# A convolution, a 2-D Fourier filter and a gate on one core: transforms in quarters of PE's array, a ring of PSUM pairs, new engine sequences

## The chip, the cores and the metric

The kernel runs on one core of one Trainium2 chip. The metric is device time in microseconds (us), the median of some executions. A core has five engines that run side by side and wait for each other by semaphores: PE (TensorE, matrix products), VectorE (DVE), ScalarE (ACT), GpSimd (POOL) and SyncE (SP, which here only starts transfers). PE reads SBUF and writes PSUM, eight banks of 2 KB on each of 128 partitions. VectorE and ScalarE read PSUM; GpSimd does not touch it in this kernel.

## What is computed

```python
x = A_u                                             # 1 x 2048 x 640
g = sigmoid((x * gate_w).sum(-1, keepdims=True))
# a: a state space convolution along time
A = -exp(log_A_real) + 1j * A_imag;  C = (C_real + 1j * C_imag) * dt[:, None]
P = exp((A * dt[:, None])[:, :, None] * pos[None, None, :])
K = 2.0 * einsum("dn,dnl->dl", C, P).real           # 640 x 2048, N = 128
a = irfft(rfft(u, 4096) * rfft(K, 4096))[:2048] + u * D_skip
# b: a filter in the 2-D Fourier domain
b = irfft2(rfft2(x) * (w_r + 1j * w_i))
return g * a + (1 - g) * b
```

The kernel gets no array of x for b apart from A_u: both branches begin with the same transform of u along time.

## The kernel before

All transforms are matrix products with tables of cosines and sines, in float32. A transform of 4096 is done in two steps, 64 by 64 with 33 residues of the first step; the 640 channels go in four groups c of 160. The program has four parts.

*The transforms of u* (`phase_a`, first half). For each c and each half h of its channels, `stage1` (L530) takes 20 tiles u[128 rows = 4 channels x 32, 64] as the weights and a block-diagonal table e1 of 128 columns as what streams past; the result of 64 columns of the array goes to the upper or the lower half of PSUM's partitions. Copies bring it to SBUF (t1). `stage2` (L543) takes 160 columns of t1 through a table w2 with 128 rows and 64 columns, again in two halves. The result is copied and stored to memory (u_d), from where both branches read it back. Between these stand the gate's products (L617), four strips of 32 columns.

*The filter b* (second half of `phase_a`), in nine rounds of 128 rows (the last one 64): `front` loads and folds rows, `transposes` (L712) turns them, `channels` multiplies with tables by `quads` (L728 with 128 rows, L726 with the 33 that are left over), `filt` multiplies with the filter on VectorE, and `back1` (L728, L726; copies L785, additions L788 and L789) and `back2` (L797, copy L798) go back. The result is stored to s3e_d.

*The convolution's kernel K* (`phase_p`, then `phase_b`). `phase_p` works out parameters from log_A_real, A_imag and so on, in 640 columns on VectorE, ScalarE and GpSimd, splits each in three bfloat16 parts (`parts`, L451 and L453) and sends them through memory (par_d). `phase_b` takes 40 steps t; each has magnitudes (products L867, exponential L868), two groups of angles (products L876, sines L882 and L888; L888 writes back into PSUM), products of both on VectorE (L896 to L898) and GpSimd (L901, L902), and 64 products in strips of 32 columns (`kgen`, L915; copy L921). Exponential and sine need different tables on ScalarE, which an ACT_TABLE_LOAD brings in.

*The convolution* (`phase_c`, `phase_d`): for each c the two steps of the transform of K (L530, copies L531; L543), the complex product with u's transform (VectorE L1027, L1028; the sums on L1033, one half on VectorE and one on GpSimd), the way back (`backs`, L1058, copy L1060, store to s3_d), and the last step, `last_e` for b (L361, L1105) and `last_c` for a (L1119, then L1122 or L1124 and L1125), with the gate, to the output. For the last c `last_c` waits for a round trip through s3_d; eight products (L1152) that nobody reads stand before it on PE.

The order of the work is written out by hand: the program is recorded as a list of operations, and `ORDER`, a list of their numbers, sets in which order each engine gets its own. A tile's place in SBUF and PSUM is chosen when its first operation is written, as the slot that has been free for longest. Before, the filter has three single PSUM banks, K's part two pairs and a bank, the convolution three pairs and two single banks.

## Time and profile before

| | us |
|---|---|
| median of 3 runs (lowest, highest) | 541.96 (538.01, 542.72) |
| the profiled execution: time, span | 540.32, 538.5 |
| PE busy (share of the span) | 479.2 (89%) |
| VectorE busy | 432.6 (80%) |
| ScalarE busy | 310.0 (58%) |
| GpSimd busy | 294.7 (55%) |
| mean granted clock of PE | 0.946 |
| moved by DMA | 101.35 MB, 188 GB/s on average |

The profile is of one execution. PE stands for its products, PEld for loading weights beside them; recorded products overlap, so a busy PE is not PE at its peak. The clock is the part of PE's full clock that was granted. "Windows" give each engine's busy time in a stretch; "groups" put together the instructions of one source line, engine and shape; the chain of waits follows the work that ended last back from the end, in pieces of start, length, what and count. A float32 product of the program stands in the trace as two records, a bfloat16 one as one.

### The profile page before, as it was taken

The page shows a single profiled execution, that of the slowest core. Times are in us where ns is not written, and L with a number is a line of the kernel's source. Part 1 is how long each engine was busy: PE and PEld are TensorE (multiplying, and loading weights), DVE is VectorE, ACT ScalarE, POOL GpSimd, SP SyncE. Part 2 cuts the span into 40 slices and gives each one's busy share as a digit, 9 for nine tenths or more (in the row PEclk, how much of TensorE's full clock was granted, in tenths as well). Part 3 has the DMA queues.
Part 4 walks back from the last instruction along what each step waited for, and adds up shares of the span by engine and source line. Part 5 has one row for each costly group of instructions (what it writes and reads, how often), then busy time and mean ns, then how long its engine had stood idle before and what let it go on. Part 6 is the DMA issues. An engine that isn't in the chain of part 4 may idle for free.

```text
span 538.5 us, 17006 instructions
## 1 busy us (share of the span) xinstructions
PE 479.2 (89%) x7288; PEld 370.3 (69%) x7288; DVE 432.6 (80%) x678; ACT 310.0 (58%) x486; POOL 294.7 (55%) x318
## 2 busy tenths in 40 slices
PE   8988999776989779997899988797899999999996
PEld 6977998554766556664676655566789878889651
DVE  4988687888898898999978987525499887999973
ACT  4682304789786878888698866866423414332110
POOL 3487430865845782763937416516455648568670
PEclk9999999779799989999899996858999999999999
DMA  8845788514126504162031360195437799799996
GB/s 328 298 179 193 274 305 279 180 51 133 51 100 191 157 27 133 37 227 87 27 103 43 110 177 1 51 367 199 147 122 254 249 393 330 248 344 280 334 302 219
DMA packets 48658, 101.35 MB, mean 188 GB/s; under 512 B 3908, under 2 KB 33368, under 8 KB 46536
## 3 DMA queue, kind: packets, MB, share of 16 engines
q1 hardware_dynamic: 25464, 67.41, 35.8%
q10 hardware_dynamic: 20080, 22.55, 13.0%
q0 software_dynamic: 3040, 10.33, 5.7%
q8 instruction: 57, 0.93, 0.7%
q14 instruction: 17, 0.14, 0.1%
HBM read 60.94 MB, written 39.65 MB: 187 GB/s over the span
## 4 chain that ended last, share of the span: by engine, by line
PE 40%; DVE 8%; ACT 7%; POOL 6%; issue 4%; DMA 3%; DVEq 0%; ACTq 0%; POOLq 0%; SPq 0%
PE psum L530 7%; PE psum L543 6%; PE psum L1058 5%; PE psum L728 5%; PE psum L915 3%; PE psum L726 3%; ACT sbuf L868 3%; PE psum L361 2%; PE psum L797 2%; PE psum L1119 2%; PE psum L876 2%; POOL sbuf L901 2%; DMA sbuf<-s3e_d 2%; ACT sbuf L882 1%; DVE sbuf L1033 1%
## 5 line engine op out<-in xcount | busy, mean ns | idle before, releaser
L543 PE MATMUL psum<-sbuf,sbuf 128*64 128x160 f32 x1056 | 87.0, 304 | 0.3 <-DVE sbuf L578 0.3
L530 PE MATMUL psum<-sbuf,sbuf 128*64 128x128 f32 x1280 | 80.1, 279 | 3.5 <-DVE sbuf L578 1.9
L530 PEld LDWEIGHTS psum<-sbuf,sbuf 128*64 128x64 f32 x1280 | 74.7, 140 | 10.2 <-issue 4.4
L543 PEld LDWEIGHTS psum<-sbuf,sbuf 128*64 128x64 f32 x1056 | 76.2, 135 | 7.4 <-issue 3.6
L1033 POOL TENSOR_TENSOR sbuf<-sbuf 64x320 f32<-64x320 f32 (+1 forms) x68 | 62.3, 918 | 33.8 <-DVE sbuf L1028 17.2
L868 ACT ACTIVATE sbuf<-psum 128x1024 f32<-128x1024 f32 (+1 forms) x80 | 61.8, 827 | 28.1 <-PE psum L867 28.0
L902 POOL TENSOR_TENSOR sbuf<-sbuf 128x512 f32<-128x512 f32 x40 | 53.6, 1342 | 34.2 <-ACT sbuf L882 23.5
L728 PE MATMUL psum<-sbuf 128*128 128x160 f32 (+3 forms) x280 | 60.1, 334 | 4.8 <-DVE sbuf L788 3.0
L901 POOL TENSOR_TENSOR sbuf<-sbuf 128x512 f32<-128x512 f32 x40 | 57.1, 1432 | 12.4 <-ACT sbuf L882 12.4
L898 DVE TENSOR_TENSOR sbuf<-sbuf,psum 128x1024 f32<-128x1024 f32 x40 | 48.6, 1215 | 15.8 <-ACT psum L888 15.7
L728 PEld LDWEIGHTS psum<-sbuf 128*128 128x128 f32 (+1 forms) x280 | 41.2, 191 | 20.6 <-issue 12.6
L915 PE MATMUL psum<-sbuf 128*32 128x64 f32 x2560 | 50.7, 238 | 5.2 <-ACT sbuf L921 1.6
L915 PEld LDWEIGHTS psum<-sbuf 128*32 128x32 f32 x2560 | 43.4, 121 | 15.7 <-issue 9.1
L1060 ACT COPY sbuf<-psum 128x640 f32<-128x640 f32 x32 | 22.2, 693 | 48.8 <-PE psum L1058 41.2
L531 ACT COPY sbuf<-psum 128x512 f32<-128x512 f32 x40 | 24.7, 623 | 43.4 <-PE psum L530 43.3
L1033 DVE TENSOR_TENSOR sbuf<-sbuf 64x320 f32<-64x320 f32 (+1 forms) x68 | 48.2, 715 | 1.1
L876 PE MATMUL psum<-sbuf 64*128 64x256 bf16 x320 | 32.6, 295 | 16.3 <-ACT sbuf L882 10.7
L888 ACT ACTIVATE psum<-psum 128x1024 f32<-128x1024 f32 x40 | 40.6, 1015 | 6.8 <-PE psum L876 6.6
L1058 PE MATMUL psum<-sbuf 128*64 128x160 f32 x528 | 42.3, 300 | 1.2 <-DVE sbuf L1033 1.1
L882 ACT ACTIVATE sbuf<-psum 128x1024 f32<-128x1024 f32 x40 | 41.0, 1026 | 3.3 <-PE psum L876 2.5
L1058 PEld LDWEIGHTS psum<-sbuf 128*64 128x64 f32 x528 | 36.7, 136 | 4.8 <-DVE sbuf L1033 1.5
L578 DVE COPY sbuf<-psum 128x320 f32<-128x320 f32 (+2 forms) x54 | 29.9, 563 | 10.4 <-PE psum L530 6.2
(145 smaller groups left out, 878.5 us busy)
## 6 DMA issues: line engine op xcount, KB each, us to landing
u_d<-sbuf SPq DMA_DIRECT2D x32, 320.0 KB, 4.5
sbuf<-u_d ACTq DMA_DIRECT2D x16, 640.0 KB, 6.5
s_d<-sbuf ACTq DMA_DIRECT2D x15, 640.0 KB, 6.2
sbuf<-s_d SPq DMA_DIRECT2D x6, 1280.0 KB, 9.3
sbuf<-in_w_l SPq DMA_DIRECT2D x8, 642.0 KB, 3.8
sbuf<-u_d SPq DMA_DIRECT2D x8, 640.0 KB, 5.1
k_d<-sbuf SPq DMA_DIRECT2D x4, 1280.0 KB, 5.7
sbuf<-k_d SPq DMA_DIRECT2D x8, 640.0 KB, 4.2
```

Source lines behind the costliest of these rows:

```text
L530: nc.tensor.matmul(p[64 * ri:64 * ri + 64, j, :], src(i + j), e1[ri], start=True, stop=True)
L543: ins = nc.tensor.matmul(p[64 * j:64 * j + 64, i, 160 * ri:160 * ri + 160], w2[:, x, 64 * ri:64 * ri + 64], t1[:, x // 2 if x < 32 else K0 ...
L728: P.matmul(out, src(c), tab[0], start=first, stop=not first)
L868: st.exp = S.activation(ef[:, :, c:c + n], p[:, :, 0:n], AF.Exp)
L876: P.matmul(p[:, j, n * g:n * g + n], pars[0][t][x, g], rp[x, c:c + n], start=True, stop=True)
L882: S.activation(sc.rearrange("p d v i -> p (d v i)"), p.rearrange("p j w -> p (j w)"), AF.Sin, scale=TWO_PI)
L898: V.tensor_tensor(out=x[:, 0].rearrange("p d (h j) -> p d h j", h=2), in0=e[:, :, 0:64].rearrange("p d (h j) -> p d h j", h=2), in1=cx.uns ...
L901: G.tensor_tensor(out=y[:, 1], in0=e[:, :, 64:96], in1=sc[:, 0], op=ALU.mult)
L902: G.tensor_tensor(out=y[:, 0], in0=e[:, :, 64:96], in1=sc[:, 1], op=ALU.mult)
L915: P.matmul(st.pb[32 * r:32 * r + 32, o, :], y[:, ri, 4 * qq + JR[r], :], x[:, ri, 4 * qq + JR[r], :], start=t % 2 + qq + 1 - ri == 0, stop ...
L1033: return eng.tensor_tensor(out=t2[64 * im:64 * im + 64, o, :], in0=m[l, :hn, 0, :], in1=m[l, :hn, 1, :], op=ALU.add if im else ALU.subtract)
L1058: T.mm = P.matmul(p[x:x + 64, i // 2, 160 * (i % 2):160 * (i % 2) + 160], T.w3[:, k0 + h + i, x:x + 64], t2[:, h + i, :], start=True, stop ...
```

## The change

- `stage1`: the weights are 64 rows (two pairs of channels, not four channels), what streams past is 64 columns of e1 without the zero blocks. Four products, for two row halves and two column halves, stand next to each other: the quarters of the array. Row halves write different banks of a pair. One copy takes up to 1024 columns.
- `stage2` and `backs`: 64 rows in place of 128, the real and the imaginary part one after the other into the same PSUM, four quarters next to each other. In `fronts` the complex product's sums are formed on all 128 partitions, the real part on VectorE, the imaginary part on GpSimd.
- `last_e`, `last_c`: 64 rows and 32 columns, eight products next to each other, without the zero blocks.
- The filter: three chunks of 64 rows in two halves in place of 128 and 33, all products, transposes and the way back with row halves. `back1` multiplies both rows at once, its copies take 644 columns, and the additions of L788 and L789 come after `back2`, as two operations of 640 columns a round.
- PSUM: until the convolution begins one pool of three pairs of banks serves everything, with two single banks for K and the gate; the convolution has four pairs.
- `phase_p`: GpSimd's operations go to VectorE, the casts to ScalarE; the gate's weights (L590) to VectorE.
- 221 products of 128 columns of weights by 128 columns and 52 of 32 by 128, into a PSUM bank that nobody reads, are put between others on PE by the order (`SPARE`).
- A new `ORDER`. The host lays out inputs and tables to match.

```diff
-    for i in range(0, nq, 4):
-        n = min(4, nq - i)
-        p = ps.tile([128, 4, 128], F32, tag="ps", name="p_s1")
-        for j in range(n):
-            for ri in range(2):
-                nc.tensor.matmul(p[64 * ri:64 * ri + 64, j, :], src(i + j), e1[ri], start=True, stop=True)
+    for i in range(0, 20, 8):
+        n = min(8, 20 - i)
+        p = pair(T, "p_s1")
+        for q in range(n):
+            for h in range(2):
+                r = slice(64 * h, 64 * h + 64)
+                for y in range(2):
+                    nc.tensor.matmul(p[64 * y:64 * y + 64, h, 64 * q:64 * q + 64], src[r, i + q, :], T.e1[y][r], start=True, stop=True)
...
+    for ro in range(2):
         for ri in range(2):
-            for j in range(nl // 64):
...
+                    nc.tensor.matmul(p[64 * j:64 * j + 64, y, 160 * ro:160 * ro + 160], T.w2[r, pr // 2, j, ri, ro, :],
+                                     t1[r, 2 * (pr // 2) + j if x < 32 else K0 // 2, :, ri], start=not ri or x == 32, stop=ri == 1 or x == K0)
...
+        def products(st, src, w, xs, name):
+            p = pair(T, name)
+            for i, x in enumerate(xs):
+                for k in range(3):
+                    for c in range(2):
+                        r = slice(64 * c, 64 * c + 64)
+                        P.matmul(p[:st.nl, c, 161 * i:161 * i + 161], src[r, k, x, 0:st.nl], td[r, w, k, :], start=k == 0, stop=k == 2)
...
-                eng.tensor_copy(t[:, j], v[:, :, :])
+                S.copy(t[:, j], v[:, :, :])
...
+            V.tensor_tensor(out=t2[:nl, x, 0], in0=ma[:nl, :hn, 0], in1=ma[:nl, :hn, 1], op=ALU.subtract)
+            G.tensor_tensor(out=t2[:nl, x, 1], in0=mb[:nl, :hn, 0], in1=mb[:nl, :hn, 1], op=ALU.add)
...
+        p = pair(T, name)
+        for j in range(2):
+            r = slice(64 * j, 64 * j + 64)
+            for g in range(4):
+                P.matmul(p[32 * g:32 * g + 32, j, 0:160 * n], w(g)[r], t3[r, a0(g):a0(g) + n], start=True, stop=True)
...
+        spare = T.p1.tile([128, 2, 128], F32, tag="pg", name="p_f")
+        for i, (cols, count) in enumerate(SPARE):
+            for _ in range(count):
+                for x in range(0, 128, cols):
+                    nc.tensor.matmul(spare[x:x + cols, i, :], c1[:, x:x + cols], c1[:, 128:256], start=True, stop=True)
...
+SPARE = (128, 221), (32, 13)
```

What the new order does is seen on the engines. PE in the filter's part; before, two calls of `quads` follow each other (L728 with 128 rows, L726 with 33):

```order
L728 MATMUL psum_72<-sbuf_68 128x160
L728 MATMUL psum_72<-sbuf_68 128x161
L726 MATMUL psum_72<-sbuf_68 128x160
L726 MATMUL psum_72<-sbuf_68 128x161
L726 MATMUL psum_72<-sbuf_68 128x160
L726 MATMUL psum_72<-sbuf_68 128x161
L728 MATMUL psum_72<-sbuf_68 128x160
L728 MATMUL psum_72<-sbuf_68 128x161 x2
L728 MATMUL psum_72<-sbuf_68 128x160
```

and after the change (L695 are the filter's products, L863 K's strips, L816 the magnitudes, L399 the unread products):

```order
L695 MATMUL psum_72<-sbuf_68 128x161 x12
L399 MATMUL psum_72<-sbuf_66 128x128
L863 MATMUL psum_72<-sbuf_68 32x64 x32
L816 LDWEIGHTS sbuf_67
L816 MATMUL psum_72<-sbuf_67 128x512
L816 LDWEIGHTS sbuf_67
L816 MATMUL psum_72<-sbuf_67 128x512
L399 MATMUL psum_72<-sbuf_66 128x128 x2
L695 MATMUL psum_72<-sbuf_68 128x161 x12
```

A call of `products` is one run of twelve in one mode of the array, and unread products in another mode stand between what had stood side by side.

ScalarE in the middle of K's steps, before (L882 and L888 are sines, L868 exponentials, the others copies):

```order
L882 ACTIVATE sbuf_68<-psum_72 128x1024
L785 COPY sbuf_68<-psum_72 128x160
L785 COPY sbuf_68<-psum_72 128x161
L888 ACTIVATE psum_72<-psum_72 128x1024
L882 ACTIVATE sbuf_68<-psum_72 128x1024
L921 COPY sbuf_67<-psum_72 128x512
L746 COPY sbuf_68<-psum_72 128x2x160
L746 COPY sbuf_68<-psum_72 128x2x161
L888 ACTIVATE psum_72<-psum_72 128x1024
L868 ACT_TABLE_LOAD
L868 ACTIVATE sbuf_68<-psum_72 128x2x512
```

and after (L830 and L836 are sines, L817 exponentials):

```order
L836 ACT_TABLE_LOAD
L836 ACTIVATE psum_72<-psum_72 128x1024
L830 ACTIVATE sbuf_68<-psum_72 128x1024
L738 COPY sbuf_68<-psum_72 128x644
L836 ACTIVATE psum_72<-psum_72 128x1024
L817 ACT_TABLE_LOAD
L817 ACTIVATE sbuf_68<-psum_72 128x2x512
L753 COPY sbuf_68<-psum_72 128x644
L817 ACTIVATE sbuf_68<-psum_72 128x2x256
L868 COPY sbuf_67<-psum_72 128x512
L836 ACT_TABLE_LOAD
```

Sines and exponentials stood in long runs and now alternate: the program has 45 table loads on the lines of exponential and sine where it had 18, and the copies are fewer and longer. In the changed order K's last steps and the filter's last round also stand side by side to the end, where before five of K's steps came after the filter.

## Prediction

> **What bounds the kernel now.** I read the windows first, cut at the three places where the work changes its kind: the transforms of u (to 96 us), the filter and the kernel K side by side (96 to 380), the convolution (380 to 520), and the way out. Each row gives the busy time of PE, weight load, VectorE, ScalarE and GpSimd, then PE's granted clock, the DMA share and GB/s.

> ```profile
> span 538.5 us, 17006 instructions
> DMA  8845788514126504162031360195437799799996
> 0.00:96.00 96.00, 87.79 (x1524) 79.95 (x1525) 70.62 (x112) 42.75 (x79) 44.81 (x48) 1.00 0.75 267
> 96.00:380.00 284.00, 243.75 (x3879) 171.31 (x3879) 231.44 (x365) 223.03 (x339) 162.16 (x174) 0.90 0.35 114
> 380.00:520.00 140.00, 134.25 (x1858) 114.35 (x1848) 122.37 (x182) 43.57 (x70) 84.56 (x95) 1.00 0.82 278
> 520.00:538.50 18.50, 13.46 (x50) 4.71 (x48) 8.21 (x20) 0.63 (x1) 3.15 (x3) 0.99 0.69 240
> 96.00:345.00 249.00, 214.27 (x3435) 148.92 (x3435) 220.52 (x349) 199.05 (x304) 151.02 (x163) 0.92 0.31 98
> 345.00:380.00 35.00, 29.49 (x456) 22.39 (x452) 10.92 (x16) 23.99 (x36) 11.14 (x11) 0.73 0.61 229
> ```

> Stages 1 and 3 are PE's: 91% and 96% busy, nothing else above 87%. Stage 2 is nobody's alone: to 345 us VectorE is busiest with 220.5 of 249 (89%), PE 86%, ScalarE 80%, and its last 35 us, when the filter has ended and K has not, keep VectorE at 31%. In stage 3 transfers take 0.82 of the DMA engines, and in the slices from about 430 us on the DMA digits are mostly 9, so they stand right behind PE.

> PE's real cost of a product is the cadence in the chain of waits (start, length, what, count), since recorded ends overlap. The groups give the counts; a float32 product of the program is two records.

> ```profile
> 390.22 0.87 PE psum L530 x16
> 391.09 1.61 PE psum L361 x8
> 392.70 1.14 PE psum L543 x16
> 393.84 1.09 PE psum L1058 x16
> 268.52 1.27 PE psum L797 x4
> 278.56 0.74 PE psum L728 x4
> 279.30 0.75 PE psum L726 x8
> 272.41 1.03 PE psum L915 x64
> L543 PE MATMUL psum<-sbuf,sbuf 128*64 128x160 f32 x1056 | 87.0, 304 | 0.3 <-DVE sbuf L578 0.3
> L530 PE MATMUL psum<-sbuf,sbuf 128*64 128x128 f32 x1280 | 80.1, 279 | 3.5 <-DVE sbuf L578 1.9 <-ACT sbuf L578 1.6
> L1058 PE MATMUL psum<-sbuf 128*64 128x160 f32 x528 | 42.3, 300 | 1.2 <-DVE sbuf L1033 1.1
> L361 PE MATMUL psum<-sbuf,sbuf 128*64 128x480 f32 (+1 forms) x96 | 20.3, 523 | 0.6 <-DMA sbuf<-s3e_d 0.6
> L1119 PE MATMUL psum<-sbuf,sbuf 128*64 128x480 f32 (+1 forms) x96 | 21.2, 528 | 2.7 <-DVE sbuf L1033 1.1 <-DVE sbuf L1122 0.5 <-DVE sbuf L1105 0.5
> ```

> So 54.4 ns each for L530, 71 for L543, 68 for L1058, 201 for L361 with 480 columns. L728 fills the array with 160 columns, L797 with 320: the second 160 columns cost 0.53 us for four, 0.13 each, and 0.21 us of a block of L728 is left for coming into its mode. L726 uses half the rows: two run at once, 94 ns. L915 uses 32 columns of the array: four run at once, 16.1 ns for 64 columns. Halves by rows and strips by columns thus run together here; no row shows both at once.

> **The change, part by part.** *First transforms in quarters* (L530, now line 525). The block-diagonal right side went, half of which was zeros: 2560 records of 64 columns take the place of 1280 of 128. Nearest row: L915, four at once, 64 columns, 16.1 ns. 2560 x 16.1 = 41.2 us against 1280 x 54.4 = 69.6: 28.4 less, half in stage 1 and half behind it. *Second transforms and the way back* (L543, L1058) do the same arithmetic in twice as many halves: 2048 at 35.5 = 72.7 against 75.0, and 1040 at 34 = 35.4 against 35.9; 2.8 less. *Last transforms* (L361, L1119) drop zeros too: eight at once in place of two, 384 records, 128 in each group at 50 ns and 64 at 33.5, 17.1 against 34.3 (64 x 201 + 32 x 135, twice): 17.2 less. Bounds for these: if four quarters take f times the time I give them, the four lines make 149.3 f + 17.1 against 214.8, so from f = 1.32 on PE gains nothing. I take f = 1, as L726 and L915 both do all that their share of the array allows.

> Stage 1 has 14.2 + 1.2 = 15.4 us less on PE. Its transfers need 0.75 x 96 = 72 us, which is under 80, so they cut a part only: I take 12, bounds 0 and 15.4. Stage 3 has 14.2 + 1.2 + 0.5 + 17.2 = 33 less: 107 on PE. But its transfers are 0.82 x 140 = 115 us of the DMA engines, with the same bytes, and at its start little can be moved. I take 124, 16 less; bounds 6 less (they stay at the digits of 430 to 513 us, where little room is left) and 33. VectorE, 122 of the 140 us now, would stand in the way at 124, but this part is halved too: 68 operations on 64 partitions become 36 on 128 with the same columns, and GpSimd's like them.

> ```profile
> L1033 DVE TENSOR_TENSOR sbuf<-sbuf 64x320 f32<-64x320 f32 (+1 forms) x68 | 48.2, 715 | 1.1
> ```

> 36 x 0.715 = 26 against 48: VectorE keeps 100 us. The last 18.5 us, a round trip through memory and the last products, stay.

> *Parameters off GpSimd.* A subtraction of 640 columns costs GpSimd 1.6 us and VectorE 0.9; the casts go to ScalarE. They lie in stage 1, where VectorE has 25 us free and ScalarE 53.

> ```profile
> L453 POOL TENSOR_TENSOR sbuf<-sbuf,sbuf 128x640 f32<-128x640 f32 (+1 forms) x4 | 6.3, 1575 | 0.3
> L453 DVE TENSOR_TENSOR sbuf<-sbuf 128x640 f32<-128x640 f32 (+1 forms) x4 | 3.4, 865 | 0.0
> 63.33 3.20 POOL L856 DMA_DIRECT2D sbuf<-par_d  x6 [3.85 <-DMA par_d<-sbuf]
> 80.08 0.50 PE L867 MATMUL psum<-sbuf 48*128 48x512 bf16 x4
> ```

> The parameters are read back from 63 us and first used at 80, 17 us of cover. A stage that is 12 shorter eats most of it, and the quicker chain gives some back: nothing, with 5 us as the upper bound.

> *Filter in 64-row halves.* Products: 280 + 280 records become 864 of L726's kind, 57 us (66 ns without the block's 0.21) against 55.6, so no gain in arithmetic. But the two sorts no longer alternate: with transposes and the way back in the same mode, stage 2 has 85 changes of mode against 271, before the unread products are added. VectorE loses 68 small operations and gets 18 of 640 columns:

> ```profile
> L788 DVE SCALAR_TENSOR_TENSOR sbuf<-sbuf,sbuf,psum 128x160 f32<-128x160 f32 x34 | 12.3, 376 | 12.3 <-ACT sbuf L785 11.7 <-PE psum L797 0.5
> L789 DVE SCALAR_TENSOR_TENSOR sbuf<-sbuf,sbuf,psum 128x160 f32<-128x160 f32 x34 | 12.1, 376 | 4.8 <-ACT sbuf L785 4.0 <-PE psum L876 0.8
> L1028 DVE TENSOR_TENSOR sbuf<-psum,sbuf 128x640 f32<-128x640 f32 (+1 forms) x36 | 28.0, 779 | 4.6 <-PE psum L543 4.3
> ```

> 18 x 0.78 = 14 against 24.4; the rest of its filter handles about as many columns as before. VectorE: 231 - 10 = 221.

> *New sequences.* ScalarE's order is where they cost. Exponentials and sines each need their own table, and the order now alternates far more: 45 table loads (22 + 6 + 17) against 18.

> ```profile
> L868 ACT ACT_TABLE_LOAD x8 | 10.3, 1283 | 1.4 <-PE psum L867 1.3
> L882 ACT ACT_TABLE_LOAD x6 | 7.7, 1283 | 0.3 <-PE psum L876 0.3
> L888 ACT ACT_TABLE_LOAD x4 | 5.1, 1283 | 0.1
> L715 ACT COPY sbuf<-psum 128x512 f32<-128x512 f32 (+3 forms) x27 | 15.0, 587 | 3.7 <-PE psum L712 3.7
> L717 ACT COPY sbuf<-psum 128x512 f32<-128x512 f32 (+3 forms) x27 | 15.0, 576 | 4.1 <-PE psum L712 3.7
> L746 ACT COPY sbuf<-psum 128x320 f32<-128x320 f32 (+3 forms) x18 | 7.7, 430 | 6.3 <-PE psum L728 6.1
> L785 ACT COPY sbuf<-psum 128x160 f32<-128x160 f32 (+1 forms) x34 | 9.2, 296 | 16.3 <-PE psum L728 16.3
> L798 ACT COPY sbuf<-psum 128x320 f32<-128x320 f32 x34 | 14.1, 434 | 4.9 <-PE psum L797 4.7
> L882 ACT ACTIVATE sbuf<-psum 128x1024 f32<-128x1024 f32 x40 | 41.0, 1026 | 3.3 <-PE psum L876 2.5
> L1060 ACT COPY sbuf<-psum 128x640 f32<-128x640 f32 x32 | 22.2, 693 | 48.8 <-PE psum L1058 41.2
> ```

> 27 x 1.283 = 34.6 us more. The filter's copies are 61.0 us now and become, a round, two of 1024 columns (1.03), two of 512 (0.59) and four of 644 (0.69): 6.0, nine times 54, 7 less. ScalarE in stage 2: 223 + 35 - 7 = 251 us, and it becomes the busiest engine there. At the 89% that VectorE reached, 251 / 0.89 = 282. The filter's rounds now end with K's last steps, so the thin 35 us go; that gain is what pays for the loads. Stage 2: 2 less, bounds 33 less (ScalarE never waits) and 28 more (loads and copies all on the path).

> *Unread products*: 442 records of 128 columns at 0.106 us and 104 at a quarter of it, 50 us, in 65 places of PE's order; 114 changes of mode come with them, 199 in all, still 72 fewer than before, 15 us at 0.21. PE in stage 2: 244 + 50 - 15 - 5 (first transforms that stand there) + 1 = 275 of 282. They cost nothing only while PE would have waited, and it is idle for 40 us there now. Behind each stand, in PE's order, products that ScalarE waits for. Against that stands the clock: 0.73 in the last 35 us, 0.90 over the stage. [...] I take 0.

> *PSUM ring*: three pairs of banks serve about 250 uses in stage 2, 3.4 us for a use at 282 us; a block of PE (0.75) and a copy (0.7 to 1.03) hold a pair for 1.8. Taken at 0; from 1.6 us of extra holding on it would bound, with no room left.

> The sum: 540.3 us (the profiled execution; its span is 538.5, the median of the three times 541.96) - 12 - 2 - 16 = 510.

> **Rivals.** *A, transfers don't hold PE* in stages 1 and 3: all of 15.4 and 33 arrives, 540.3 - 48.4 - 2 = 490. For it: the digits leave room before 430 us. Against: the 9s behind it. *B, the table loads lie bare*: stage 2 grows by 28 in place of losing 2, 540. For: ScalarE runs in order, at 251 of 284 us. Against: its 61 idle us. *C, the unread products fall on the path*: 275 of work and the 40 of waiting, stage 2 takes 315, 31 more than now, 543. For: ten in a row are 2 us ahead of a wanted product. Against: they stand where waits were expected. *D, four quarters run only two at a time* (the change doesn't do what it says): f = 2, PE's four lines take 316 for 214.8, 101 more, 640; it decides from f = 1.32 and is the slower one. Against: L726 and L915. For: no row has both splits.

> **How the numbers follow.** Forecast 0.55, A 0.20, B 0.12, C 0.08, D 0.05. Forecast and A are faster by over 1% (about what a measurement can tell), B and C lie at no change, a quarter of them to either side: faster 0.80, same 0.10, slower 0.10. The range runs from 485, a little below A since ScalarE's load allows more, to 535, short of B and C: what it leaves out is most of B and C, D, and a part of A. The forecast's own range is 497 to 524.

> **What would show it.** Line 525 at about 16 ns a record in the chain, 541 at 35; DMA digits of 9 through stage 3 and PE under 90% there; ScalarE over 85% in stage 2 with 45 loads; first angles some 10 us earlier. Wrong if stage 2 is under 265 or over 300 us, or if stage 3 falls below 115.

## The result and the profile after

The kernel after the change takes 584.7 us (median of four executions, 582.4 to 588.6) against 540.0 (536.9 to 542.7): ratio 1.084, 95% interval 1.075 to 1.093. It is 45 us slower; the forecast was 30 us faster. The profiled execution took 588.6 us, its span is 586.5. From its page: the busy tenths of PE, PE's clock and the DMA engines in 40 slices.

```profile
span 586.5 us, 24840 instructions
PE   6886978999998978899998998966888669687692
PEclk9888899999999799999999999988899969988887
DMA  8666468433226305151214123584966989999995
```

PE had 7s to 9s nearly everywhere before; now it has 6s in the first slices and, from slice 27 of the 40 on, 6s again and again, mostly beside DMA digits of 8 and 9. The same windows as in the prediction (PE, weight load, VectorE, ScalarE, GpSimd, PE's clock, DMA share, GB/s), cut where the three stages meet:

```profile
0.00:89.00 89.00, 69.00 (x2365) 61.60 (x2369) 45.89 (x75) 44.73 (x64) 10.63 (x24) 0.90 0.65 226
89.00:385.00 296.00, 271.41 (x5258) 215.55 (x5252) 245.08 (x326) 254.48 (x301) 156.71 (x148) 0.99 0.36 114
385.00:586.00 201.00, 145.70 (x3772) 115.39 (x3760) 99.15 (x149) 43.06 (x60) 56.59 (x59) 0.88 0.85 238
```

From here on the stages are cut at two events that every trace has, the first sine of K's steps and the end of the last one, and "the end" is what follows the last product of the way back. All in us:

| kernel | stage 1 | stage 2 | stage 3 | of it the end |
|---|---|---|---|---|
| before | 97.5 | 283.9 | 157.2 | 19.7 |
| after | 90.7 | 295.0 | 200.8 | 28.8 |

So stage 1 gave 7, stage 2 lost 11, stage 3 lost 44. Stage 3 is not longer because PE has more to do: it is busy for 146 of 201 us. Its clock is lower, too: 0.90 and 0.88 in stages 1 and 3, where it had been 1.00. Added up, PE stands at half clock for 17 us of stage 1 and 48 of stage 3, where it had been 0 and under 1, and most of these stretches begin in or just behind a pause (391.2 to 398.0 us, 408.2 to 411.7, 466.3 to 479.9).

**Two things show in stage 3.** The first is in the groups of PE and in the chain of waits (start, length, what).

```profile
L541 PE MATMUL psum<-sbuf,sbuf 64*64 64x160 f32 x2048 | 103.9, 321 | 21.6 <-issue 20.4
L525 PE MATMUL psum<-sbuf,sbuf 64*64 64x64 f32 x2560 | 57.4, 239 | 27.3 <-issue 22.1
```

```profile
402.69 1.21 PE psum L525 x80
403.89 4.28 issue
408.18 0.58 PE psum L525 x12
408.76 0.08 PE psum L541
408.86 3.64 PE psum L541 x62
```

PE stops for 4.3 us in the middle of a run of the same products and waits for nothing that the profile knows ("issue"). The before lines of these products had 0.3 and 3.5 us of idle time, none of it "issue". What PE waits for shows in the DMA queue of kind "instruction", q8 (packets, MB, share of the DMA engines' time). First the page of the kernel before, then after:

```profile
q1 hardware_dynamic: 25464, 67.41, 35.8%
q8 instruction: 57, 0.93, 0.7%
```

```profile
q1 hardware_dynamic: 26120, 67.36, 37.8%
q8 instruction: 89, 1.46, 1.1%
```

After, PE has 11374 products (counted here and below as records of the trace, of which a float32 product is two) and as many weight loads, 22748 instructions; 1.46 MB is 64 bytes for each, and a packet of 16 KB holds 256, that is 128 products. Before it is the same sum: 14576 instructions, 57 packets. By this sum I take these packets to be PE's own program. Set beside six of PE's pauses, from the packets and the records of the trace after (us; PE stops where the last record before the pause starts):

```
PE stops   resumes   a packet of q8 starts, lands   landed before PE resumes
 388.31    393.48      391.09      392.06             1.41
 403.68    408.18      405.67      406.58             1.59
 418.55    420.99      418.33      419.71             1.28
 463.96    469.91      467.14      468.45             1.46
 510.27    514.72      512.11      513.45             1.27
 543.11    547.88      544.95      546.30             1.58
```

Counting every pause of 0.6 us or more that ends 1.15 to 1.75 us behind such a landing: 19 us in stage 1 and 42 us in stage 3, against 0 and 1 in the kernel before. The places fit as well: from one of these pauses to the next in stage 3 PE works through 127 or 128 products or about a whole multiple (255, 510, 765); 15 of the 16 pauses stand so. Two packets never start closer than 3.39 us in this trace, that is 26.5 ns for each of its 128 products (3.42 us before, and 3.22 in wide_tiles, the closest pair of any run). The quarters of line 525 follow each other at 18.4 ns within a run: they use up 128 in 2.4 us, faster than any two packets came. I call this **theory F**, fetches.

The long pauses need more than that. In five of the six above the packet starts only 1.8 to 3.2 us after PE has stopped, and 7 to 11 us behind the packet before it. In these stretches the DMA engines are busy for 0.83 or more with other transfers. So the packet may be waiting behind them; no run shows that by itself.

The second is in the transfers: q1 above moved the same 67.4 MB in 222 us of the 16 engines' time (37.8% of 586.5) instead of 193. The DMA issues (KB each, median us to landing), before and after:

```profile
sbuf<-s_d SPq DMA_DIRECT2D x6, 1280.0 KB, 9.3
```

```profile
sbuf<-s_d SPq DMA_DIRECT2D x6, 1280.0 KB, 18.3
```

These are the loads of `load_c`. The change cut them, and those of `load_e`, by partitions, which the diff shown above leaves out:

```diff
-        nc.sync.dma_start(t3es[c][:, :, :], T.s3e_d[c].rearrange("k (r a) d -> (k r) a d", r=4))
+        for g in range(4):
+            nc.sync.dma_start(t3es[c][32 * g:32 * g + 32], T.s3e_d[c, :, 16 * g:16 * g + 16])
...
-            for x in range(2):
-                nc.sync.dma_start(t3[:, x], src[:, x])
+            for j in range(2):
+                nc.sync.dma_start(t3[64 * j:64 * j + 64], T.s3_d[c, :, 32 * j:32 * j + 32])
```

Their packets of 10 KB took 426 ns on average before and 641 after, those of 20 KB (10 KB twice) 1443. In stage 3 q1 and q10, the queues of SP and ScalarE, took 161 us of the engines' time instead of 119. Not all of that is slower packets: behind K's last sine these queues start 44.3 MB of transfers, and 40.2 before, since some that stood ahead of it (a load of s3e_d among them) now come later. This is **theory T**, transfers. **Theory U** is what the prediction doubted in stage 2: unread products or table loads.

### The profile page after: what moved, and what is told of

Same layout as the page of the kernel before. It is cut to its first block, busy times and chain, and to the rows that moved or that the text cites. A ratio compares the mean times of both kernels' runs of the same rounds, so it can differ in the third digit from the quotient of the medians.

```text
span 586.5 us, 24840 instructions
## 1 busy us (share of the span) xinstructions
PE 486.1 (83%) x11374; PEld 392.5 (67%) x11374; DVE 390.1 (67%) x548; ACT 342.3 (58%) x424; POOL 223.9 (38%) x231
## 3 DMA queue, kind: packets, MB, share of 16 engines
q1 hardware_dynamic: 26120, 67.36, 37.8%
q8 instruction: 89, 1.46, 1.1%
## 5 line engine op out<-in xcount | busy, mean ns | idle before, releaser
L541 PE MATMUL psum<-sbuf,sbuf 64*64 64x160 f32 x2048 | 103.9, 321 | 21.6 <-issue 20.4
L541 PEld LDWEIGHTS psum<-sbuf,sbuf 64*64 64x64 f32 x2048 | 83.9, 140 | 34.2 <-issue 26.4
L525 PE MATMUL psum<-sbuf,sbuf 64*64 64x64 f32 x2560 | 57.4, 239 | 27.3 <-issue 22.1
L525 PEld LDWEIGHTS psum<-sbuf,sbuf 64*64 64x64 f32 x2560 | 54.3, 152 | 31.2 <-issue 23.5
L695 PE MATMUL psum<-sbuf 64*128 64x161 f32 (+1 forms) x864 | 69.1, 307 | 2.7 <-ACT sbuf L817 0.8
L399 PE MATMUL psum<-sbuf 128*128 128x128 f32 (+1 forms) x546 | 69.3, 286 | 0.0
L695 PEld LDWEIGHTS psum<-sbuf 64*128 64x128 f32 (+1 forms) x864 | 61.7, 184 | 8.7 <-ACT sbuf L817 2.3
L817 ACT ACTIVATE sbuf<-psum 128x1024 f32<-128x1024 f32 (+1 forms) x80 | 62.0, 817 | 5.6 <-PE psum L816 5.1
L399 PEld LDWEIGHTS psum<-sbuf 128*128 128x128 f32 (+1 forms) x546 | 56.5, 175 | 10.5 <-issue 8.6
L978 PE MATMUL psum<-sbuf 64*64 64x160 f32 x1040 | 51.1, 312 | 4.4 <-issue 3.2
L957 DVE TENSOR_TENSOR sbuf<-psum,sbuf 128x640 f32<-128x640 f32 (+1 forms) x36 | 27.9, 778 | 38.4 <-PE psum L541 32.1
L958 DVE TENSOR_TENSOR sbuf<-psum,sbuf 128x640 f32<-128x640 f32 (+1 forms) x36 | 28.1, 780 | 37.7 <-PE psum L541 22.6
L575 ACT COPY sbuf<-psum 128x1024 f32<-128x1024 f32 (+3 forms) x42 | 33.1, 808 | 31.7 <-PE psum L525 17.8
L863 PE MATMUL psum<-sbuf 128*32 128x64 f32 x2560 | 46.8, 226 | 3.0 <-POOL sbuf L850 1.1
L978 PEld LDWEIGHTS psum<-sbuf 64*64 64x64 f32 x1040 | 41.7, 139 | 9.8 <-issue 5.3
L863 PEld LDWEIGHTS psum<-sbuf 128*32 128x32 f32 x2560 | 39.9, 113 | 12.0 <-issue 7.4
L526 ACT COPY sbuf<-psum 128x1024 f32<-128x1024 f32 (+1 forms) x24 | 21.1, 913 | 40.4 <-PE psum L525 24.7
```

The lines of the kernel that those rows point to most:

```text
L399: nc.tensor.matmul(spare[x:x + cols, i, :], c1[:, x:x + cols], c1[:, 128:256], start=True, stop=True)
L525: nc.tensor.matmul(p[64 * y:64 * y + 64, h, 64 * q:64 * q + 64], src[r, i + q, :], T.e1[y][r], start=True, stop=True)
L541: nc.tensor.matmul(p[64 * j:64 * j + 64, y, 160 * ro:160 * ro + 160], T.w2[r, pr // 2, j, ri, ro, :], t1[r, 2 * (pr // 2) + j if x < 32 el ...
L575: return (V.tensor_copy if T.dve and dst.home.name == "ut" else S.copy)(dst, src)
L695: P.matmul(p[:st.nl, c, 161 * i:161 * i + 161], src[r, k, x, 0:st.nl], td[r, w, k, :], start=k == 0, stop=k == 2)
L817: S.activation(ef[:, :, c:c + n], p[:, :, 0:n], AF.Exp)
```

## The experiments

Medians; "before" was run beside each on the same chip (536 to 541 us). Stages as above, from each kernel's profile; the profiled executions of after, before_split, copy_for_exp and before_straddle lie 3 to 8 us above their medians, so differences between profiles can be that much larger or smaller than those of the medians. "Gaps" are the pauses behind fetches in stages 1 and 3, by the rule above, to about 1 us. The rule can catch another wait by chance: all 9 us of before_part_loads and about half of the 6 of before_split end at a transfer or another engine that the profile names.

| kernel | median (range) | stages 1, 2, 3 | gaps |
|---|---|---|---|
| after | 584.7 (582.4-588.6) | 90.7, 295.0, 200.8 | 19, 42 |
| wide_tiles | 577.5 (575.1-580.1) | 84.4, 293.8, 194.8 | 12, 13 |
| no_unread | 603.2 (601.2-605.7) | 89.2, 313.8, 200.7 | 20, 38 |
| u_loads_on_sync | 590.7 (587.8-592.5) | 91.7, 294.4, 200.8 | 23, 44 |
| before_split | 559.2 (553.8-563.1) | 110.2, 285.7, 165.4 | 8, 6 |
| full_loads | 766.8 (763.0-773.6) | 90.5, 293.7, 376.9 | 22, 22 |
| wide_full_loads | 760.2 (757.7-767.1) | 85.0, 294.9, 378.6 | 12, 14 |
| before_part_loads | 566.1 (564.7-569.3) | 98.8, 280.0, 185.5 | 0, 9 |
| copy_for_exp | 575.9 (570.4-581.9) | 91.1, 282.4, 203.4 | 22, 41 |
| before_strided_loads | 589.0 (586.1-594.3) | 97.5, 284.2, 202.6 | 0, 0 |
| two_queues | 584.9 (581.7-588.1) | 89.7, 297.1, 196.1 | 21, 27 |
| wide_two_queues | 576.5 (575.5-577.5) | 85.8, 293.4, 194.1 | 13, 24 |
| before_unread | 546.3 (543.8-549.9) | 99.3, 286.6, 158.5 | 1, 2 |
| row_order | 568.0 (564.7-570.7) | 89.3, 295.2, 180.5 | 20, 29 |
| wide_row_order | 558.2 (556.2-559.0) | 84.0, 293.4, 176.7 | 12, 18 |
| before_quarters | 543.7 (538.4-547.0) | 99.1, 279.1, 165.3 | 1, 6 |
| before_straddle | 550.0 (547.6-557.6) | 99.8, 286.8, 169.1 | 0, 0 |

### Fewer, larger products: wide_tiles

```diff
-            e1[i, r, :, r % 2] = kr[:32].reshape(8, 2, 2, 2, 32)[:, i].reshape(16, 2, 32).transpose(2, 0, 1)
+            e1[i, r, :, r % 2] = kr[:32].reshape(16, 2, 2, 32)[:, :, i].transpose(2, 0, 1)
...
-                    nc.tensor.matmul(p[64 * j:64 * j + 64, y, 160 * ro:160 * ro + 160], T.w2[r, pr // 2, j, ri, ro, :],
-                                     t1[r, 2 * (pr // 2) + j if x < 32 else K0 // 2, :, ri], start=not ri or x == 32, stop=ri == 1 or x == K0)
+                    nc.tensor.matmul(p[64 * j:64 * j + 64, y, 160 * ro:160 * ro + 160], T.w2[:, x, 64 * ro:64 * ro + 64],
+                                     t1[:, x // 2 if x < 32 else K0 // 2, :, x % 2], start=True, stop=True)
...
-                        for x in (0, 64) if pr < 16 else (0,):
-                            P.matmul(p[x:x + 64, j, 160 * i:160 * i + 160], T.w3[r, pr, im, x:x + 64], t2[r, h + i, im], start=im == 0, stop=im == 1)
+                        n = 128 if pr < 16 else 64
+                        P.matmul(p[0:n, j, 160 * i:160 * i + 160], T.w3[r, pr, im, 0:n], t2[r, h + i, im], start=im == 0, stop=im == 1)
```

> The changed kernel (profiled 588.6 us) with the same multiplications in fewer, larger pieces: the second transforms (line 541) over the whole 128 rows with real and imaginary parts stacked (1056 records instead of 2048), the way back (line 978) in two 64-row halves of 128 columns (520 instead of 1040). PE's arithmetic, every transfer and every other instruction stay. Theory F (PE is starved of instructions: in the changed kernel's trace eleven gaps of 1.5 to 6 us in 380-550 us, 38 us together, end 1.3 to 1.6 us after one of the 16 KB instruction fetches has landed): stage 3 has about 1000 records and 8 fetches fewer, the gaps fall below 15 us, the time to 545-565 us. Theory T (the data transfers and the queues they are issued from hold stage 3): transfers are unchanged, 579-590 us. Theory U (the unread products or ScalarE's table loads hold stage 2): unchanged, 579-590 us.

The gaps in stage 3 fell from 42 to 13 us as F says, but the time only by 7 (between the two profiled executions by 13, 6 in stage 1 and 6 in stage 3), and F had expected 20 at least. Where the 29 us went shows in the chain of waits of wide_tiles and in its last window:

```profile
456.22 5.72 ACTq L950
...
489.85 19.69 DMA s_d<-sbuf
...
530.07 16.65 DMA s_d<-sbuf
```

```profile
378.00:573.00 195.00, 150.33 (x2766) 110.34 (x2765) 99.41 (x148) 42.52 (x60) 56.44 (x59) 0.89 0.85 244
```

ScalarE, PE and the loads now wait for transfers, and the DMA share stays at 0.85. So the gaps were there, but most of their time is taken by other waits once they go.

### More, smaller products in the kernel before: before_split

Each of these products is written out as `parts` products of its columns:

```diff
-                nc.tensor.matmul(p[64 * ri:64 * ri + 64, j, :], src(i + j), e1[ri], start=True, stop=True)
+                nc.tensor.matmul(p[64 * ri:64 * ri + 64, j, :], src(i + j), e1[ri], start=True, stop=True, parts=2)
...
+                    w = a[2].shape[1] // parts
+                    b = [a[0][:, i * w:i * w + w], a[1], a[2][:, i * w:i * w + w]]
```

> The kernel before (540 us) with every product of its first and second transforms and its way back cut into two products of half the columns, one behind the other: the same arithmetic in 2864 records more (10150 instead of 7288). Theory F: stage 3 goes from 1888 to about 3100 records (15 to 24 fetches), gaps that end behind a fetch appear, 10 to 40 us longer: 550-580 us. Theories T and U: nothing that they name is changed, 540 us within 1%.

1.034 (1.026 to 1.043) of before, as F expected. Gaps behind fetches appear, 8 us in stage 1 and about 3 in stage 3, where there had been none. That is not all of the 21 us: PE's busy time in stages 1 and 3 also grew by 14 (97 and 152 us against 88 and 148), so two halves cost PE more than the whole.

### Stage 2: no_unread, before_unread, copy_for_exp

> The changed kernel without the unread products of line 399 (546 records left out, nothing else). Theory U (they lie on stage 2's path): stage 2 is 10 us shorter and the time about 575 us. Theory F (instruction fetches starve PE in stages 1 and 3): those stages have the same records as before, so the time stays within 1% of 584 us, or grows a little if the granted clock of stage 2 falls under its 0.99. Theory T: unchanged.

> The kernel before with 86 unread products (128 rows by up to 128 columns, into the PSUM region that the next product overwrites) ahead of 33 products in stage 2 that PE reached 0.75 us or more after the one before. no_unread said that the changed kernel's unread products are worth 18 us, with the granted clock of stage 2 at 0.99 with them and 0.87 without; the kernel before has 0.90 there. If that is the clock: stage 2's clock rises to 0.95 or more and the time falls by 3 to 12 us (528-537). If the unread products help in the changed kernel for another reason, or hold the products behind them up here: 540 us or more.

> The changed kernel with the exponentials of line 817 replaced by plain copies (AF.Copy): the magnitudes, and with them the output, are not the reference's; it leaves out the exponential so that ScalarE's function tables need not alternate. 45 table loads of 1283 ns in stage 2 fall to a few. If the table loads are on stage 2's path (rival B of the prediction), stage 2 gets shorter by up to 50 us, at least 20; if ScalarE has room for them, by less than 5 us. Stages 1 and 3 stay as they are.

Windows of stage 2, of no_unread, before_unread and copy_for_exp in this order:

```profile
89.00:403.00 314.00, 234.04 (x4732) 178.68 (x4731) 245.18 (x325) 254.82 (x302) 154.49 (x149) 0.87 0.33 108
```

```profile
96.00:386.00 290.00, 251.35 (x4072) 180.52 (x4071) 232.33 (x367) 226.38 (x344) 164.44 (x176) 0.98 0.35 115
```

```profile
89.00:375.00 286.00, 267.24 (x5343) 214.67 (x5338) 249.88 (x328) 202.65 (x259) 159.69 (x150) 0.99 0.37 120
```

Without the unread products the changed kernel is 18.5 us slower, 19 of it in stage 2, where PE's clock falls from 0.99 to 0.87: they pay, and theory U falls for them. Such filling in the kernel before, with 86 products of the program at other places, raised its clock from 0.90 to 0.98 and still cost 1.6% (1.012 to 1.021). One reading is that a higher clock is worth something only where PE sets the time: PE is at 271 of 296 us in the changed kernel and at 244 of 284 in the one before. But the 86 can also have held up the products behind them, and no run separates the two. For the table loads U holds in part. The groups of the changed kernel:

```profile
L817 ACT ACT_TABLE_LOAD x22 | 28.2, 1283 | 9.1 <-PE psum L816 5.8 <-DVE sbuf L575 3.0
L836 ACT ACT_TABLE_LOAD x17 | 21.8, 1283 | 8.8 <-DVE sbuf L575 4.3 <-PE psum L824 3.0 <-issue 1.3
L830 ACT ACT_TABLE_LOAD x6 | 7.7, 1283 | 0.1
```

With 43 of these 45 gone ScalarE has 52 us less to do and stage 2 is 12.6 us shorter; PE is then busy for 267 of its 286. That is less than the 20 I had named for "on the path" and more than the 5 for "room enough".

### Transfers by part of the partitions: before_part_loads, before_strided_loads, before_straddle

The kernel before, its loads written out as several transfers each: neighbouring partitions (first line), the same counts with every fourth or second partition (second line), and three pieces, 32 to 95, 0 to 31 and 96 to 127 (third line).

```diff
+                b = a if parts == 1 else [x[i * w:i * w + w] for x in a]
...
+                b = a if parts == 1 else [x[i::parts] for x in a]
...
+                lo, hi = ((0, 128), (32, 96), (0, 32), (96, 128))[i + (parts > 1)]
```

> The kernel before with its loads of the last transforms cut by partitions: load_e into four transfers of 32 partitions, each half of load_c (first three channel groups) into two of 64 partitions. Same bytes, packets of 10 KB as before. Theory T: these packets go from 429 to about 600 ns, DMA engines get 10 to 20 us more work in stage 3, 545-560 us. Theory F: 540 us within 1%.

> The kernel before with the same loads cut into as many transfers as in before_part_loads (load_e in four, each half of load_c in two), but each transfer writes every fourth or every second partition instead of 32 or 64 neighbouring ones. Bytes, packets (10 KB) and counts of transfers are those of before_part_loads (566 us). If neighbouring partitions make the packets slow: packets return to about 430 ns and the time to 540 us within 1.5%. If the number of transfers or of packets in each makes them slow: 650-690 ns a packet as in before_part_loads, 560-570 us.

> The kernel before with the loads of before_part_loads cut otherwise: each of load_e and of the halves of load_c into partitions 32 to 95, 0 to 31 and 96 to 127, three transfers of neighbouring partitions, same bytes and 10 KB packets. If it matters only how few partitions a transfer writes, or how many transfers there are: 15% or so of the packets under 450 ns, as in before_part_loads, mean near 680, 560-570 us. If the lower 64 and the upper 64 partitions are written through ways of their own, so that a transfer across the middle runs at full rate: about half of the packets take about 400 ns and half 650 to 800, mean near 550, and the time lies between 540 and 566, near 550.

Packets of 10 KB behind 360 us, from the traces (ns; share of those up to 430):

```
                        mean   median   share
before                   426     385     0.83
before_part_loads        677     721     0.15
before_straddle          565     486     0.43
before_strided_loads     454     385     0.78
```

Cutting alone, without one instruction of the change on PE, costs 5.6%: 1.056 (1.051 to 1.061), 30 us against the runs beside it, and stage 3 is 28 us longer. With one piece laid across the middle 43% of the packets are fast again, and the time, 550.0, lies where it was expected. The packets' mean is 565 ns against 677 in before_part_loads, though here too the pieces have 64 and 32 partitions. Which partitions a transfer writes matters in these runs, not only how few, or how many transfers there are. The strided cut says the same by its packets, but its time is useless for this: other engines wait for those loads there and not in the kernel before, as the waits of its VectorE show, so it seems to have added dependencies.

```profile
DVE sbuf L1039 <- DMA sbuf<-s3e_d: 22.1, 2, 11.9
DVE sbuf L1033 <- DMA sbuf<-s3e_d: 10.5, 1, 10.5
```

How few partitions a transfer writes does not order the packets by itself: in before_part_loads those to 32 partitions took 623 ns and those to 64 took 713 (split by when the loads ran), where all 128 took 426. The share of fast packets rose from 0.15 to 0.43 with the piece 32 to 95. Why a piece across the middle is faster, by ways of their own for the two halves or otherwise, no run shows.

### The same on the changed kernel: full_loads, row_order and both with wide_tiles

full_loads writes all 128 partitions by one transfer, from a source of two blocks (load_c) or four (load_e); row_order loads the rows in the order of the kernel before (the last group's load_c stays cut, and the weights are not reordered to match). Of load_c, first the changed kernel, then full_loads, then row_order:

```diff
-            for j in range(2):
-                nc.sync.dma_start(t3[64 * j:64 * j + 64], T.s3_d[c, :, 32 * j:32 * j + 32])
+            for x in (0, 16):
+                nc.sync.dma_start(t3[:, x:x + 16].rearrange("p x d -> p (x d)"), T.s3_d[c].rearrange("k (j x) d -> j k x d", j=2)[:, :, x:x + 16].rearrange("j k x d -> j k (x d)"))
...
+                nc.sync.dma_start(t3[:, x:x + 16], T.s3_d[c].rearrange("k (j x) d -> (k j) x d", j=2)[:, x:x + 16])
```

> The changed kernel with the loads of its last transforms written over all 128 partitions by each transfer: load_e as one transfer instead of four of 32 partitions, load_c as two of 128 partitions and 16 rows instead of two of 64 partitions and 32 rows (for the last 160 channels, five of 32 partitions spread over all 128 instead of ten of 16). Same bytes. Theory T (the transfers of stage 3 became slower because each writes few partitions: packets of 10 KB took 641 ns in the changed kernel and 429 ns before, 20 KB packets 1446 ns): 10 KB packets return to about 430 ns, the engines of DMA lose about 30 us of work in stage 3, and the time falls to 555-570 us. Theory F alone (instruction fetches hold PE, transfers don't matter): within 5 us of 584, gaps behind fetches still about 40 us. Both, F on top of T: the gaps stay near 35 us and the time falls by less than 15 us.

> Both edits on the changed kernel: second transforms over 128 rows and way back in two 64-row halves (1500 PE records fewer; alone it took the gaps behind instruction fetches in stage 3 from 43 to 13 us but the time only from 584 to 577 us), and the loads of the last transforms over all 128 partitions. Theory T+F (two causes one on top of the other, each hidden when the other is taken away): 530-545 us, more than the sum of the two edits alone. Theory F alone: no more than 5 us below the 577 us of the first edit. Theory T alone: the same time as the loads alone give, within 5 us.

> The changed kernel with the loads of the last transforms (load_e, and load_c of the first three channel groups) in the row order of the kernel before: all 128 partitions and packets of 10 KB in each transfer, same bytes. The rows then stand in another order than the weights of the last transforms expect, so those products, and the output, are not the reference's; their number and shape stay. Theory T (slow packets hold stage 3): 10 KB packets at about 430 ns, DMA engines lose 30 to 40 us of work in stage 3, the time falls by 10 to 30 us, to 555-575. Theory F above T (gaps behind fetches hold PE just as long): the gaps stay at about 40 us, the time within 8 us of 584.

> row_order and wide_tiles together (the output is not the reference's, for the row order alone). If slow packets and gaps behind fetches are all of the loss in stage 3, each hidden when the other goes: stage 3 comes back to 155-165 us, the time to 533-548 us. If something else holds stage 3 as well (the order of the sequences, ScalarE's issues): 555-575 us.

The first pair missed by 200 us. Its packets are fast (458 ns), but while a load_c of this form runs, packets of q1 keep only 1.9 of the 16 engines busy, and 3.9 during a load_e: about as many as the source has blocks, two and four. PE's waits in stage 3 of full_loads:

```profile
PE psum L1023 <- DMA sbuf<-s_d: 102.9, 4, 36.0
PE psum L1023 <- DMA sbuf<-s3e_d: 40.6, 2, 24.6
```

row_order is the clean form. 10 KB packets are at 462 ns, q1 and q10 need 132 us of the engines' time in stage 3 for the same 44.3 MB that took 161, and the time falls by 17 us, 20 in stage 3. The gaps fall with it, from 42 to 29 us, though PE's program is the same. With wide_tiles the time falls by 26 in all, not to the 540 I had hoped for. That is about the sum of the two edits alone (17 and 7), so slow packets alone are not what hid the gaps in wide_tiles; what did stays open. The last windows of row_order and of wide_row_order:

```profile
385.00:565.00 180.00, 138.60 (x3758) 109.78 (x3757) 97.30 (x148) 42.28 (x59) 55.67 (x59) 0.93 0.78 263
```

```profile
378.00:554.00 176.00, 144.07 (x2745) 107.65 (x2733) 98.40 (x148) 42.64 (x59) 55.74 (x58) 0.94 0.79 268
```

Of the 44 us, 20 go with the loads' form, packets and the gaps that fall with them, and 4 more with wide_tiles. Of the 19.5 that stay, 9 are the end (28.8 us against 19.7). The timeline of the kernel after shows what stands there (start, length, what):

```profile
554.97 3.91 SPq L1001 DMA_DIRECT2D sbuf<-s3e_d  x3
567.98 2.96 DVE L1041 TENSOR_TENSOR sbuf<-psum,sbuf 128x960 f32<-128x960 f32 x3 [11.87 <-issue]
569.22 5.90 POOL L1042 TENSOR_TENSOR sbuf<-sbuf 128x960 f32<-128x960 f32 x3 [14.19 <-DVE sbuf L1041]
570.85 2.96 DVE L1028 TENSOR_TENSOR sbuf<-psum,sbuf 128x960 f32<-128x960 f32 x3
```

The last steps of channel group 2 (L1041, L1042) and the filter's last step of group 3 (L1001, L1028) come behind the last way back; the kernel before has them in front of it. The other 10 us lie ahead of the end, where wide_row_order still has 18 us of gaps behind fetches, most of them in the products of line 525, and the 4 MB more of transfers; which of them makes the 10 was not tried.

### What did not help: u_loads_on_sync, two_queues, before_quarters

The edits of u_loads_on_sync, of two_queues (load_e likewise), and of before_quarters in stage 3:

```diff
-        nc.scalar.dma_start(st.us[:nl, 0:gn], T.u_d[c, :nl, g0:g0 + gn])
+        nc.sync.dma_start(st.us[:nl, 0:gn], T.u_d[c, :nl, g0:g0 + gn])
...
-                nc.sync.dma_start(t3[64 * j:64 * j + 64], T.s3_d[c, :, 32 * j:32 * j + 32])
+                (G if j else nc.sync).dma_start(t3[64 * j:64 * j + 64], T.s3_d[c, :, 32 * j:32 * j + 32])
...
+                    a = [(p[64 * ri:64 * ri + 64, h, 64 * j:64 * j + 64].rearrange("p (b x) -> p b x", b=2), src(i + j)[64 * h:64 * h + 64],
+                          e1[ri][64 * h:64 * h + 64].rearrange("p (b h x) -> p b h x", b=2, h=2)[:, :, h]) for h in range(2)]
+                    nc.tensor.matmul(*a[0], *a[1], start=True, stop=True)
```

> The changed kernel with the 20 loads of line 946 (u_d to SBUF in stage 3) issued from SyncE's queue instead of ScalarE's. Theory T, in the form that ScalarE's copies stand behind DMA issues that do not come off (five issues of 3.1 to 6.9 us on ScalarE, 24.7 us together, in the changed kernel's trace): 10 to 15 us faster, about 570-575 us. Theory F: PE's gaps behind instruction fetches stay at about 38 us in stage 3, the time falls by no more than 5 us.

> The changed kernel with the second half of each load_c (partitions 64 to 127, first three channel groups) and the second and fourth quarter of each load_e issued from GpSimd's queue, so that transfers to different partitions can be under way together. Same bytes and transfers. Theory T (neighbouring partitions make packets slow, because all 16 engines write the same few): the 20 KB packets fall from 1446 ns towards 900, the time by 5 to 20 us, to 565-580. Theory F alone: within 5 us of 584.

> The two edits wide_tiles (1500 PE records fewer, 577 us alone) and two_queues together. Theory T+F, two causes one on top of the other: the sum of both edits or more, 545-567 us. If the transfers stay slow from two queues as well: 575-580 us.

> The kernel before with the first transforms of stage 3 (channel groups 1 to 3) in quarters of PE's array and all else as it was: its loads over all 128 partitions, its second transforms and way back in whole rows. 480 records more (2368 instead of 1888 in stage 3, 19 fetches in 158 us), their arithmetic 10 us less. If quarters help where fetches keep up and the packets are fast: 3 to 8 us faster, 530-536 us. If fetches or the DMA engines take it back: 538 us or more.

Taking the u loads off ScalarE made it no faster (590.7 us), so ScalarE's long issues do not set the time here. From two queues the 20 KB packets stay at 1365 ns, and both kernels take what they take from one (584.9 and 576.5). In two_queues the gaps of stage 3 are 27 us, not 42, and the time is the same: gaps that go are not time won. before_quarters puts line 525's form into stage 3 of the kernel before, where packets are fast and a fetch comes every 8 us on average: 1.006 (1.002 to 1.011), no gain. Stage 2 is 5 us shorter and stage 3 is 8 longer, with 5.5 us of gaps behind fetches and PE only 3 us less busy; what takes the rest back was not settled. No version beat the kernel before.

## Why the prediction was wrong

- **The step that failed**: "its transfers are 0.82 x 140 = 115 us of the DMA engines, with the same bytes". The bytes of the whole kernel are the same, but not the time per byte, and stage 3 got 4.2 MB more of them. The loads were recut by partitions, their packets of 10 KB take 1.5 times as long (641 ns for 426), and the queues of SP and ScalarE need 161 us for stage 3 in place of 119; with the packets fast again it is 132. Stage 3 shrinks by 20 us when the cut alone is undone (row_order), and that of the kernel before grows by 28 when the cut alone is made (before_part_loads). The forecast of 16 less went by bytes. What kept these 16 away is not shown: even wide_row_order has 177 us in stage 3, with PE busy for 144 of 176 and a DMA share of 0.79.
- **A term was missing**: the cost of a product's own instructions. 4086 more products were costed by their arithmetic. That came out 10 to 15% dearer: line 525 goes at 18.4 ns in runs (forecast 16.1), 541 at 39.0 (35.5), 978 at 37.4 (34), so four quarters do run at once and rival D is out, but at these paces the three lines make about 166 us, where the sum had 149 against 180.5 before: half of that gain was not there, and why the pace is slower was not tried. And 128 products of line 525 pass in 2.4 us, while no two packets of their program start closer than 3.2. Hence stage 1 gave 7 in place of 12; with 1500 products fewer it gives 13.
- **"The last 18.5 us, a round trip through memory and the last products, stay"**: the end grew by 9 us, since the order leaves work of two channel groups behind the last way back.
- **Stage 2, 2 less**: 11 more. ScalarE's load was right (251 forecast, 254.5 measured), but it does not reach 89% there, only 86%; copy_for_exp puts the table loads at 12.6 us, between the forecast and rival B (28); without the loads stage 2 takes 282.4, which the forecast had given it with them. VectorE has 245 us, not 221, which no run shows to matter.
- **Unread products at 0**: they are worth 18.5 us, so rival C has the wrong sign. The clock is what is seen to change with them (0.99 against 0.87). The prediction weighed the clock of before, 0.73 and 0.90, against their cost and took 0; what filled gaps do to the clock no row of before showed.
- **The marks**: 18 ns, DMA digits of 9 (mostly from slice 34 on), 45 table loads and ScalarE over 85% came true or near it and told nothing, since the forecast had no mark for a longer stage 3. Parameters and the PSUM ring were not tested apart.
- **A slip that changes little**: of the 640 records of first transforms that the sum puts behind stage 1, 160 stand in stage 2, where the prediction takes 5 us off PE again. So 3 to 4 us of PE's 33 less in stage 3 are counted twice.

## What to carry to other kernels

Cost a transfer by the packets of the same shape in the trace, not by its bytes: packets of 10 KB took 426 ns before and 641 after. Look at which partitions it writes (677 ns in before_part_loads, 565 in before_straddle) and at the first dimension of its source (1.9 engines busy with two blocks in full_loads). Cutting products into smaller ones multiplies the instructions that must be fetched (57 packets became 89); compare 128 products' time (2.4 us on line 525) with the distance of two packets of the instruction queue (3.39 us and more in the kernel after) before counting the gain, and take that distance from a stage where the DMA engines are as busy as they will be. When a removed wait moves the time little (29 us of gaps for 7), read which resource stands high under it (here the DMA share, 0.85) and undo both; here that gave 26 of the 45 us.
